# A gated attention followed by a multiplicative FFN: up products of the last three blocks in twenty products of parts

## The chip, the core and the metric

The kernel runs on one core of a Trainium2 chip. The metric is the device time of one execution in microseconds, the median of several runs. The names of the engines are those of the profile: PE is TensorE, DVE is VectorE, ACT is ScalarE, POOL is GpSimd, SP is the queue that issues the DMAs.

## The reference

All inputs are float32: q, k, v and f_logit of shape (4, 8, 768, 48), w1 and w2 of 384 x 1024, w3 of 1024 x 1024, w_out of 1024 x 384.

```python
f = 1.0 / (1.0 + np.exp(-f_logit))
for t in range(S):
    state = f[:, :, t, :, None] * state + np.einsum('bhd,bhe->bhde', k[:, :, t], v[:, :, t])
    y[:, :, t] = np.einsum('bhd,bhde->bhe', q[:, :, t], state)
x = attn_out.transpose(0, 2, 1, 3).reshape(B * S, H * D)   # 3072 x 384
h = ((x @ w1) * (x @ w2)) @ w3
return h @ w_out
```

## The kernel before

**Attention.** The 3072 tokens are 24 units of 128. Per unit VectorE makes two scans over the gates (L393, L415) and scales q and k (L409, L430); TensorE makes scores (L456) and transposes of k (L468); ScalarE copies the scores out of PSUM, GpSimd masks them (L549), TensorE multiplies with v (L490) and with the state (L509), makes the state's increment (L523), and VectorE updates the state (L638 to L644). The result is written to DRAM (L684) and gathered, transposed, into xt (L687). A unit's chain goes over four engines, so the gaps of TensorE in it are filled with products of the FFN.

**FFN.** The 24 units make six blocks of 512 tokens. w3 and w_out are multiplied into one matrix wc (L1176) early on. For each block, x is cut into 3 x 2 parts: three 128-row slices of the 384 features, two halves of 256 tokens. w1 and w2 are each cut into 3 x 8 tiles of 128 x 128. The function `seven` takes two of the eight column tiles and one of the two matrices: four outputs of 128 x 256 would take twelve products, and seven combinations of parts (m1 to m7, as Strassen's scheme does for a 2 x 2 x 2 part of it, with the third slice of features added in the plain way) make it eleven. Its sums are made by VectorE out of PSUM: u2 (L838), u3 (L841), c11, c22, c21, c12 (L847, L852), and for w2 the multiplication with the result of w1 (L856); ScalarE copies m1 (L817). The sums of parts of x (`sums`, L784) and of w (`sum_up`, L1208) are made on VectorE. Block 0 and half of block 1 use plain products (`part`). Every block ends in two `down` groups, each of seven combinations of four products of 192 columns, with four sums S0 to S3 before them (L950), and u2, u3, c22, c21, c12 after (L965, L978, L989, L995, L1003). All products go through `three` (L714), so they stand under one line in the profile.

**Order.** `Plan` takes every step with an engine, an assumed cost, a priority and its dependencies, and puts out a list for each engine; the hardware queues run in that order. `need(u)` is the due time of unit u. PSUM is two banks for scores (pa), two for values (py), and a pool of four banks, f, for the rest. A step that takes a bank names the step that frees it. After the last unit, a range check on VectorE (L1233 to L1241) decides whether a general path is to be taken at the end; it is not taken here.

Of the kernel before, what the change touches and what calls it, by code (L numbers as in the profile page):

```python
# [64 lines left out]
LOW = float.fromhex("0x1p-15")  # L67
HIGH = float.fromhex("0x1.dffffep+16")
LOOSE = 5
FULL = 35.0  # L70
FLOOR = 2.0**-60
RANGE = 2.0**-40


class Plan:
# [26 lines left out]
    def order(self):  # L102
# [12 lines left out]
        def places(t, name):  # L115

            ends = [(after(t, enders[id(h)]) if h else 0.0, i) for i, h in enumerate(self.pools[name])]
            return [e for e in ends if e[0] is not None]
# [88 lines left out]
def ranged(ctx, tc, q, k, f_logit, v, w1, w2, w3, w_out, out, ident, w12, wc, left):  # L207
# [7 lines left out]
    work = ctx.enter_context(tc.tile_pool(name="work", bufs=2))  # L215
    work3 = ctx.enter_context(tc.tile_pool(name="work3", bufs=3))
    abp = ctx.enter_context(tc.tile_pool(name="abp", bufs=4))
    outs = ctx.enter_context(tc.tile_pool(name="outs", bufs=4))
    one = ctx.enter_context(tc.tile_pool(name="one", bufs=1))
    dram = ctx.enter_context(tc.tile_pool(name="dram", bufs=3, space=bass.MemoryType.DRAM))  # L220
# [3 lines left out]
    floor = keep.tile([R, NQ], F32, name="floor")  # L224
    back = keep.tile([R, NQ], F32, name="back")
    gate = [keep.tile([R, NQ + 1], F32, name=f"gate{i}") for i in range(2)]
    qs, ks, fs = ([keep.tile([R, NQ], F32, name=f"{nm}{i}") for i in range(n)] for nm, n in (("q", 3), ("k", 2), ("f", 2)))
    masked = [keep.tile([P, 2, HP, C], F32, name=f"A{i}") for i in range(2)]
    sb = [keep.tile([R, HP, R], F32, name=f"sb{i}") for i in range(2)]
# [51 lines left out]
    def heads(t):  # L281
        return t.rearrange("p (h c) -> p h c", c=C)
# [44 lines left out]
    def need(u):  # L327
        return (0.0, 1.0, 2.0, 3.0)[u] if u < 4 else 60 + 14.5 * (u - 4)

# [22 lines left out]
    def front(u):  # L352
# [38 lines left out]
        def forward():  # L391
            s["P"] = one.tile([R, NQ], F32, name="fwd")
            nc.vector.tensor_tensor_scan(s["P"], gate[u % 2][:, 0:NQ], floor, 0.0, ALU.mult, ALU.max)  # L393
# [19 lines left out]
        def backward():  # L413
            s["R"] = one.tile([R, NQ], F32, name="bwd")
# [6 lines left out]
        def scale_k():  # L421
            s["K"] = work.tile([R, NQ], F32, name="K")
# [165 lines left out]
    def rest(u):  # L588
# [68 lines left out]
        def outcome():  # L657
            s["ys"] = work3.tile([R, HP, C], F32, name="ys")
# [51 lines left out]

    def three(out_, lhs, rhs, start=True):

        for i in range(len(lhs)):
            nc.tensor.matmul(  # L714
                out_, lhsT=lhs[i], rhs=rhs[i], start=start and i == 0, stop=i == len(lhs) - 1,
                skip_group_check=True,
            )

    def ffn(n):
# [187 lines left out]

        if n == 0:
            part(0, 2, range(KH))
# [10 lines left out]
        def down(i):  # L920
# [89 lines left out]

            n0 = 100 * n + 90 + i + 60 * (n > 1) + 30 * (n == NB - 2)

# [246 lines left out]
    for u in range(NU):  # L1259
# [363 lines left out]
```

## Time and profile before

| | |
|---|---|
| median of 3 runs | 490.2 us (490.07 to 490.37) |
| profiled execution | 490.37 us, its span 488.7 us |
| TensorE's granted clock | 0.998 |
| busy: PE, DVE, ACT, POOL | 477.4, 359.8, 166.2, 61.5 us |
| last unit's products with v begin | 298.13 us |
| last product's sum begins | 483.23 us |
| products through L714 of 256 columns, mean of a record | 0.379 us |
| products through L714 of 192 columns, mean of a record | 0.327 us |
| DVE sums 128x256 with a PSUM input (L852) | 0.42 us |
| DVE sums 128x512 from SBUF (L950) | 0.68 to 0.69 us |
| POOL masks 64x256 (L549), 80 of them | 0.578 us |

The page has one execution on the hardware. The share of busy time of each engine is given for the whole and for 40 slices of the span, as tenths. The chain is followed back from the last instruction to what released it. A product in float32 is two records on PE, and records overlap, so what a product costs is to be read from the starts of neighbouring records and not from a record's mean. "Idle before" is named with the engine whose instruction ended it.

### The profile page before, as it was taken

How to read it: one execution, taken by the hardware profiler on the slowest of the kernel's cores; microseconds unless marked ns; L12 is line 12 of the kernel's file. 1: busy time of each engine (PE TensorE's matmuls, PEld its weight loads, DVE VectorE, ACT ScalarE, POOL GpSimd, SP SyncE). 2: the span in 40 equal slices, each digit the busy share in tenths (PEclk: the TensorE clock that was granted, in tenths of full speed). 3: DMA queues.
4: the chain of work that ended last, by engine and by line, in shares of the span. 5: the costliest groups of instructions: out<-in, count | busy, mean ns of one | idle time of the engine just before them, and what ended most of it. 6: DMA issues, size and time to landing. Idle time of an engine off the chain costs nothing.

```text
span 488.7 us, 9559 instructions
## 1 busy us (share of the span) xinstructions
PE 477.4 (98%) x3696; PEld 408.0 (83%) x3696; DVE 359.8 (74%) x721; ACT 166.2 (34%) x380; POOL 61.5 (13%) x115
## 2 busy tenths in 40 slices
PE   7899999999999999999999999999999999999995
PEld 6788744666799888899988888988899888889994
DVE  7999899999997688688877866456763667655541
ACT  4688456573234442544433541001100110110010
POOL 9110000305202111221311201000000000000000
PEclk9999999999999999999999999999999999999999
DMA  5999367663326653346642113000011000000011
GB/s 176 297 334 262 100 243 258 211 184 82 82 79 166 164 138 106 90 124 165 166 124 51 34 25 91 32 34 0 20 48 50 16 1 0 1 1 1 32 62 43
DMA packets 44920, 50.00 MB, mean 102 GB/s; under 512 B 15426, under 2 KB 34370, under 8 KB 43842
## 3 DMA queue, kind: packets, MB, share of 16 engines
q1 hardware_dynamic: 44866, 49.30, 34.3%
q8 instruction: 31, 0.51, 0.4%
q14 instruction: 23, 0.19, 0.1%
HBM read 40.63 MB, written 8.65 MB: 101 GB/s over the span
## 4 chain that ended last, share of the span: by engine, by line
PE 86%; DVE 6%; issue 1%; DVEq 0%
PE f L714 69%; PE f L1176 4%; PE py L490 4%; PE pa L456 2%; PE py L509 2%; PE py L468 2%; DVE place L1208 1%; PE f L523 1%; DVE place L1123 1%; DVE place L1129 1%; DVE bwd L415 1%; PE f L692 1%; DVE fwd L393 1%; DVE place L1222 0%; DVE place L950 0%
## 5 line engine op out<-in xcount | busy, mean ns | idle before, releaser
L714 PE MATMUL f<-xt,w 128*128 128x256 f32 (+1 forms) x600 | 159.1, 396 | 0.0
L714 PEld LDWEIGHTS f<-xt,w 128*128 128x128 f32 x600 | 113.5, 190 | 24.7 <-issue 10.8
L714 PE MATMUL f<-place 128*128 128x192 f32 (+1 forms) x504 | 112.1, 350 | 0.3 <-DVE place L950 0.3
L714 PEld LDWEIGHTS f<-place 128*128 128x128 f32 x504 | 87.8, 190 | 6.4 <-DVE place L950 0.6
L549 POOL TENSOR_SCALAR_AFFINE_SELECT A<-A 64x256 f32<-64x256 f32 (+1 forms) x84 | 49.0, 604 | 232.1 <-PE py L468 106.0
L1176 PE MATMUL f<-place 128*128 128x384 f32 x128 | 42.6, 489 | 0.5 <-DVE place L1129 0.5
L817 ACT COPY a<-f 128x256 f32<-128x256 f32 x36 | 13.4, 373 | 81.5 <-PE f L714 69.6
L1176 PEld LDWEIGHTS f<-place 128*128 128x128 f32 x128 | 23.9, 190 | 17.3 <-DVE place L1129 1.1
L714 PE MATMUL f<-xt,place 128*128 128x256 f32 x144 | 37.1, 380 | 0.0
L714 PE MATMUL f<-wc,ab 128*128 128x192 f32 x192 | 35.1, 326 | 0.0
L714 PEld LDWEIGHTS f<-wc,ab 128*128 128x128 f32 x192 | 32.0, 190 | 0.4
L393 DVE TENSOR_TENSOR_SCAN fwd<-gate,floor 112x512 f32<-112x512 f32 x24 | 29.9, 1244 | 2.5 <-ACT gate L385 2.0
L543 ACT COPY A<-pa 64x256 f32<-64x256 f32 (+1 forms) x60 | 24.2, 439 | 20.2 <-PE pa L456 19.6
L415 DVE TENSOR_TENSOR_SCAN bwd<-gate,back 112x512 f32<-112x512 f32 x24 | 29.6, 1233 | 0.7
L714 PEld LDWEIGHTS f<-xt,place 128*128 128x128 f32 x144 | 26.6, 189 | 3.5 <-issue 0.2
L841 DVE TENSOR_TENSOR place<-f,a 128x256 f32<-128x256 f32 x36 | 15.2, 421 | 18.7 <-PE f L714 18.5
L653 ACT COPY sb<-S 48x192 f32<-48x192 f32 x40 | 14.0, 350 | 27.7 <-DVE S L644 18.2
L490 PEld LDWEIGHTS py<-A,vt 128*64 128x64 f32 (+1 forms) x320 | 17.5, 129 | 6.7 <-issue 6.2
L1112 ACT ACTIVATE place<-place 128x512 f32<-128x512 f32 (+2 forms) x24 | 21.3, 886 | 4.0 <-DVE w L1129 2.0
L490 PE MATMUL py<-A,vt 128*64 128x128 f32 x320 | 22.6, 281 | 0.0
L714 PE MATMUL f<-place,w 128*128 128x256 f32 x72 | 21.4, 379 | 0.0
L1115 ACT ACTIVATE place<-place 128x512 f32<-128x512 uint32 (+2 forms) x24 | 21.3, 893 | 0.0
(119 smaller groups left out, 632.7 us busy)
## 6 DMA issues: line engine op xcount, KB each, us to landing
place<-in_w_dram SPq DMA_DIRECT2D x8, 1024.0 KB, 4.9
place<-in_w_dram SPq DMA_DIRECT2D x12, 512.0 KB, 9.4
out_dram<-o SPq DMA_DIRECT2D x24, 192.0 KB, 1.9
q<-in_q_dram SPq DMA_DIRECT2D x46, 96.0 KB, 2.4
f<-in_f_logit_dram SPq DMA_DIRECT2D x44, 96.0 KB, 2.3
k<-in_k_dram SPq DMA_DIRECT2D x44, 96.0 KB, 2.3
yt<-ys SPq DMA_DIRECT2D x40, 96.0 KB, 2.1
xt<-yt SPq DMA_DIRECT2D x20, 192.0 KB, 2.7
```

The costliest lines, as they stand in the source:

```text
L393: nc.vector.tensor_tensor_scan(s["P"], gate[u % 2][:, 0:NQ], floor, 0.0, ALU.mult, ALU.max)
L415: nc.vector.tensor_tensor_scan(s["R"][:, ::-1], gate[u % 2][:, NQ:0:-1], back[:, ::-1], 0.0, ALU.mult, ALU.max)
L490: nc.tensor.matmul(y_block(u, b)[64 * half : 64 * half + w], lhsT=s["v"][:, h * D : h * D + w], rhs=s["A"][:, par, hp], start=zone not in ...
L543: nc.scalar.copy(parts_of(s["A"].rearrange("p r h c -> p (r h c)"))[p0:p1, :, f], parts_of(s["pa"].rearrange("p r n -> p (r n)"))[p0:p1, : ...
L549: nc.gpsimd.affine_select(out=a, in_=a, pattern=pattern, compare_op=ALU.is_ge, fill=0.0, base=0, channel_multiplier=-1,)
L653: nc.scalar.copy(sb[u % 2][rows(par), :, 64 * par : 64 * par + D], s["S"][rows(par)])
L714: nc.tensor.matmul(out_, lhsT=lhs[i], rhs=rhs[i], start=start and i == 0, stop=i == len(lhs) - 1, skip_group_check=True,)
L817: nc.scalar.copy(q["a"], q["X"])
L841: nc.vector.tensor_tensor(ups["u3", k], q["Y"], q["a"], ALU.add)
L1112: nc.scalar.activation(m, hi.bitcast(F32), AF.Abs)
L1115: nc.scalar.activation(lo.bitcast(F32), lo, AF.Copy, bias=2.0, scale=2.0**-51)
L1176: nc.tensor.matmul(w3s["p", jc], lhsT=w3s[jc][:, kc * P : kc * P + P], rhs=wos[:, kc], start=(kc == 0), stop=(kc == KF - 1),)
```

## The change

The up products of blocks 3, 4 and 5 are no longer made by `seven`. The new function `twenty` takes one matrix (w1 or w2) and four of the eight column tiles. It sees x as 3 x 2 parts and w as 3 x 4 parts, so that eight outputs of 128 x 256 would take 24 products, and makes them with twenty. TWENTY names for each product which part or sum of x and of w it multiplies; X_SUMS and W_SUMS say how the 13 sums of x (128 x 256 each, per block) and the 23 sums of w (128 x 512 each, once) are made; both run on VectorE. STEPS lists products (p) and the sums that follow: with an operand in PSUM (a name in b) on VectorE, copies (=) on ScalarE, sums of SBUF values alone on GpSimd. Of the final multiplications of w1's result with w2's, the even outputs go to GpSimd, the odd ones to VectorE.

- These three blocks are planned behind all units of attention, and `twenty` waits for the last unit. The due times of the units are closer, 12 apart and not 14.5. The gather of block 5 is issued when block 3's products are done.
- Its results stand in five halls of PSUM: the banks of pa and py, and one bank of the pool f, which leaves three to the down groups.
- The sums lie in the places of the attention's tensors, which are joined into one tile (chunked), and of `place`. A sum of w that needs a place of the attention's waits for the attention's end; the others wait for block 2's up products, whose sums of w they overwrite.
- Attention itself, blocks 0 to 2, and all down groups are computed as before; the priorities of the down groups change.

```diff
+X_SUMS = (
+    "6 0 - 2", "7 1 - 2", "8 6 + 3", "9 3 + 4", "10 7 + 4", "11 7 - 3", "12 9 - 5", "13 6 + 1",
+    "14 8 - 5", "15 1 + 4", "16 0 + 3", "17 6 - 4", "18 10 - 5",
+)
+W_SUMS = (
+    "12 0 - 4", "13 12 + 5", "14 1 + 9", "15 13 - 1", "16 12 - 6", "17 14 - 16", "18 17 + 10", "19 12 - 14",
+    "20 11 + 3", "21 18 + 20", "22 15 + 7", "23 16 - 1", "24 22 - 3", "25 18 + 11", "26 0 + 8", "27 26 - 14",
+    "28 13 + 7", "29 19 + 7", "30 16 + 2", "31 17 - 8", "32 21 + 2", "33 19 - 20", "34 4 + 8",
+)
+TWENTY = (
+    (11, 16), (7, 12), (10, 19), (12, 23), (13, 0), (6, 24), (5, 18), (14, 25),
+    (4, 15), (9, 27), (8, 21), (13, 28), (15, 29), (3, 30), (12, 31), (16, 32),
+    (2, 33), (17, 22), (18, 17), (2, 34),
+)
+STEPS = (
+    "p b0 1 1", "= v0 b0", "p b1 4 1", "p b1 19 0", "- o0 b1 v0", "p b2 0 1", "- v1 v0 b2",
+    "p b3 17 1", "p b4 8 1", "= v2 b4", "+ v3 b3 v2", "+ v4 v3 v0", "p b5 5 1", "- v5 v3 b5",
+    "p b6 16 1", "- v6 v5 b6", "p b7 10 1", "- v7 b7 v5", "p b8 13 1", "= v8 b8", "+ v9 v8 b7",
+    "p b9 6 1", "+ v10 b9 v8", "p b9 7 0", "- o7 v7 b9", "- v11 v1 v9", "p b6 15 0", "+ o2 v11 b6",
+    "p b10 2 1", "p b11 12 1", "= v12 b10", "- v13 v12 b11", "- o3 v6 v13", "- v14 v13 v4", "p b12 11 1",
+    "+ o1 v14 b12", "p b13 18 1", "+ v15 b13 v12", "- v16 v1 v15", "+ v17 v16 v2", "p b14 3 1", "- o5 v17 b14",
+    "- o6 v10 v16", "p b15 9 1", "p b15 14 0", "+ o4 v16 b15",
+)
+LATE = 3
...
+def first_use(side, d):
+    order = [TWENTY[int(r.split()[2])][side] for r in STEPS if r[0] == "p"]
+    above = [first_use(side, int(r.split()[0])) for r in (X_SUMS, W_SUMS)[side] if str(d) in r.split()[1::2]]
+    return min([i for i, x in enumerate(order) if x == d] + above)
...
+    chunked = keep.tile([P, 23 * NQ], F32, name="chunked")
+    spots = [chunked[:, i * NQ : i * NQ + NQ] for i in range(23)]
+    floor, back, *spare = [x[0:R] for x in spots[4:]]
+    qs, ks, fs, k_in, q_in, y_in = (
+        [spare.pop() for _ in range(n)] for n in (3, 2, 2, 2, 3, 3)
+    )
+    one_p, one_r = spare.pop(), spare.pop()
+    masked = [chunked[:, 2 * i * NQ : 2 * i * NQ + 2 * NQ].rearrange("p (r h c) -> p r h c", r=2, h=HP) for i in range(2)]
...
+    w_at, after = {}, []
+    keeps = sorted({w for _, w in TWENTY if w >= 12}, key=lambda w: first_use(1, w))
+    soon = [at(2 * TH * i, 2 * TH) for i in range(12)] + spots[23 - len(spare) :]
+    w_at.update(zip(keeps, soon))
+    later = spots[: 23 - len(spare)]
+    for w in keeps[len(soon) :]:
+        w_at[w] = later.pop()
+        after.append(w)
+    ends = [at(a + 2 * TH * i, 2 * TH) for a in (9216, 12864) for i in range(2)]
+    w_at.update(zip([int(r.split()[0]) for r in W_SUMS if int(r.split()[0]) not in w_at], ends))
+    late_v = [t[:, i * TH : i * TH + TH] for t in later + ends for i in range(2)]
+    late_x = [[late_v.pop(0) for _ in X_SUMS] for _ in range(2)]
...
+    plan.pool("h", 5)
+    plan.pool("v", len(late_v))
...
-        return (0.0, 1.0, 2.0, 3.0)[u] if u < 4 else 60 + 14.5 * (u - 4)
+        return (0.0, 1.0, 2.0, 3.0)[u] if u < 4 else 60 + 12 * (u - 4)
...
-            s["Q"] = work3.tile([R, NQ], F32, name="Q")
+            s["Q"] = q_in[u % 3]
...
-        before = blk[n - 2]["up"] if n >= 2 else []
         if u < NPE:
             t["z"] = plan.add("PE", 1.6, moved, [t["y"]], n0 - 996, takes=["f"], frees=[moving])
-            t["x"] = plan.add("ACT", 0.55, settled, [t["z"]] + before, n0 - 20, frees=[t["z"]])
+            t["x"] = plan.add("ACT", 0.55, settled, [t["z"]], n0 - 20, frees=[t["z"]])
         else:
             t["z"] = moves(2, 197, 250, written, [t["y"]], n0 - 100)
-            t["x"] = moves(1, 197, 250, gathered, [t["z"]] + before, n0 - 100)
-
+            def gather():
+                t["x"] = moves(1, 197, 250, gathered, [t["z"]] + (blk[n - 2]["up"] if n >= 2 else []), n0 - 100)
+            if n < LATE + 2:
+                gather()
+            else:
+                t["gather"] = gather
+    halls, late_w, late_q = {}, [], []
+    def hall():
+        nm, i = ("pa", "py", "f")[plan.got // 2], plan.got % 2
+        if nm not in halls:
+            halls[nm] = ps.tile([P, 2, NQ], F32, name=nm)
+        return halls[nm][:, i, 0:TH]
+    def claimed():
+        halls["f"] = bank().unsqueeze(1)
+    def w_part(i, which=None):
+        if i >= 12:
+            t = w_at[i].rearrange("p (w t c) -> p w t c", w=2, t=2)
+        else:
+            kc, c = divmod(i, 4)
+            b, a = divmod(c, 2)
+            t = w12.rearrange("p w k (a b c) -> p w k a b c", b=2, c=P)[:, :, kc, 2 * a : 2 * a + 2, b]
+        return t if which is None else t[:, which]
+    def prepare():
+        ended = [tk[u]["z"] for u in range(NU - 3, NU)] + [tk[NU - 1][nm] for nm in ("v", "y", "c")]
+        halls["claim"] = plan.add("PE", 0.0, claimed, ended, 0, takes=["f"])
+        there = [x for p in pieces.values() for x in p] + blk[LATE - 1]["up"] + enders(LATE - 1)
+        tasks = {}
+        for row in sorted(W_SUMS, key=lambda r: first_use(1, int(r.split()[0]))):
+            d, x, op, y = row.split()
+            d, x, y = int(d), int(x), int(y)
+            def emit(d=d, x=x, y=y, op=op):
+                nc.vector.tensor_tensor(w_part(d), w_part(x), w_part(y), ALU.add if op == "+" else ALU.subtract)
+            tasks[d] = plan.add("DVE", 0.69, emit, [tasks[i] for i in (x, y) if i in tasks] + there + ended * (d in after), 100 * LATE + 20 + 0.01 * len(tasks))
+        return tasks
...
+        def x_sums():
+            tasks = {}
+            deps = [tk[n * UB + c]["x"] for c in range(UB)]
+            if n < LATE + 2:
+                deps += [tk[u]["z"] for u in range(NU - 3, NU)] + [tk[NU - 1][nm] for nm in "vyc"]
+            else:
+                deps += blk[n - 2]["last"]
+            for row in sorted(X_SUMS, key=lambda r: first_use(0, int(r.split()[0]))):
+                d, x, op, y = row.split()
+                d, x, y = int(d), int(x), int(y)
+                def emit(d=d, x=x, y=y, op=op):
+                    nc.vector.tensor_tensor(x_part(d), x_part(x), x_part(y), ALU.add if op == "+" else ALU.subtract)
+                tasks[d] = plan.add("DVE", 0.43, emit, [tasks[i] for i in (x, y) if i in tasks] + deps, 100 * n + 30 + 0.01 * len(tasks))
+            return tasks
+        def twenty(t, which, sums_):
+            n0 = 100 * n + 50 + 8 * t + 4 * which
+            tiles = [c + 2 * t for c in (0, 4, 1, 5)]
+            ready = [tk[n * UB + c]["x"] for c in range(UB)] + [tk[NU - 1][nm] for nm in "myv"] + [halls["claim"]]
+            last = takes_ab(tiles[0], plan.add("PE", 0.0, lambda: None, ready + late_q[-1:], n0))
+            made, homes, opened, read = {}, {}, {}, {}
+            def result(o):
+                return a_b(tiles[o % 4])[:, o // 4 * TH : o // 4 * TH + TH]
+            started = None
+            def step(row):
+                nonlocal last, started
+                kind, to, *of = row.split()
+                if kind == "p":
+                    i = int(of[0])
+                    x, w = TWENTY[i]
+                    start = of[1] == "1"
+                    def emit():
+                        if start:
+                            homes[to] = hall()
+                        lhs = w_part(w, which)[:, t] if w >= 12 else up_weights(w12, which, w // 4, tiles[w % 4])
+                        three(homes[to], [lhs], [x_part(x)], start)
+                    deps = [last, sums_.get(x), late_w[0].get(w)] + read.get(to, [])
+                    last = plan.add("PE", 0.43, emit, deps, n0, takes=["h"] if start else [])
+                    made[to] = last
+                    if start:
+                        opened[to] = last
+                    s["up"].append(last)
+                    if len(s["up"]) % len(TWENTY) == len(TWENTY) // 2:
+                        started = last
+                    return
+                here = to[0] == "o" and which == 0
+                eng = "ACT" if kind == "=" else "DVE" if "b" in of[0] + of[1] else "POOL"
+                def emit():
+                    if here:
+                        homes[to] = result(int(to[1:]))
+                    else:
+                        homes[to] = late_v[plan.got]
+                    if kind == "=":
+                        nc.scalar.copy(homes[to], homes[of[0]])
+                        return
+                    e = nc.vector if eng == "DVE" else nc.gpsimd
+                    e.tensor_tensor(homes[to], homes[of[0]], homes[of[1]], ALU.add if kind == "+" else ALU.subtract)
+                cost = {"ACT": 0.38, "DVE": 0.43, "POOL": 1.1}[eng]
+                made[to] = plan.add(
+                    eng, cost, emit, [made[i] for i in of] + ready_v, n0 - 200, takes=[] if here else ["v"],
+                    frees=[opened[i] for i in of],
+                )
+                opened[to] = made[to]
+                for i in of:
+                    read.setdefault(i, []).append(made[to])
+                if to[0] == "o":
+                    o = int(to[1:])
+                    if which == 0:
+                        first_of[t, o] = made[to]
+                    else:
+                        def times():
+                            (nc.vector if o % 2 else nc.gpsimd).tensor_tensor(result(o), result(o), homes[to], ALU.mult)
+                        s["done"][t].append(plan.add("DVE" if o % 2 else "POOL", 0.43 if o % 2 else 1.1, times, [made[to], first_of[t, o]], n0 - 190, frees=[made[to]]))
+            ready_v = ready + [tk[u]["z"] for u in range(NU - 3, NU)] + list(late_w[0].values())
+            for row in STEPS:
+                step(row)
+            late_q.append(started)
...
+        first_of = {}
+        if n >= LATE:
+            if not late_w:
+                late_w.append(prepare())
+            sums_ = x_sums()
+            for t in range(2):
+                for which in range(2):
+                    twenty(t, which, sums_)
+            s["last"] = s["up"][-1:]
+        elif n == 0:
...
-            n0 = 100 * n + 90 + i + 60 * (n > 1) + 30 * (n == NB - 2)
+            n0 = 100 * n + 90 + i + 75 * (n > 0) + 90 * (n >= LATE - 1)
...
-        if u % UB == UB - 1:
+        if u % UB == UB - 1 and u // UB < LATE:
             ffn(u // UB)
+    for n in range(LATE, NB):
+        for u in range(n * UB, n * UB + UB):
+            if "gather" in tk[u]:
+                tk[u]["gather"]()
+        ffn(n)
```

More of the change, by code (lines that the diff above doesn't have):

```diff
@@ L115, in places @@
         def places(t, name):
-            ends = [(after(t, enders[id(h)]) if h else 0.0, i) for i, h in enumerate(self.pools[name])]
+            ends = [(after(t, enders.get(id(h), [{"end": None}])) if h else 0.0, i) for i, h in enumerate(self.pools[name])]
             return [e for e in ends if e[0] is not None]
@@ L215, in ranged @@
     work = ctx.enter_context(tc.tile_pool(name="work", bufs=2))
-    work3 = ctx.enter_context(tc.tile_pool(name="work3", bufs=3))
     abp = ctx.enter_context(tc.tile_pool(name="abp", bufs=4))
     outs = ctx.enter_context(tc.tile_pool(name="outs", bufs=4))
-    one = ctx.enter_context(tc.tile_pool(name="one", bufs=1))
-    dram = ctx.enter_context(tc.tile_pool(name="dram", bufs=3, space=bass.MemoryType.DRAM))
+    dram = ctx.enter_context(tc.tile_pool(name="dram", bufs=12, space=bass.MemoryType.DRAM))
     ps = ctx.enter_context(tc.tile_pool(name="ps", bufs=1, space=PSUM))
     ps_f = ctx.enter_context(tc.tile_pool(name="ps_f", bufs=1, space=PSUM))
-    floor = keep.tile([R, NQ], F32, name="floor")
-    back = keep.tile([R, NQ], F32, name="back")
+    chunked = keep.tile([P, 23 * NQ], F32, name="chunked")
[6 more added lines that the diff above has]
+    masked = [chunked[:, 2 * i * NQ : 2 * i * NQ + 2 * NQ].rearrange("p (r h c) -> p r h c", r=2, h=HP) for i in range(2)]
     gate = [keep.tile([R, NQ + 1], F32, name=f"gate{i}") for i in range(2)]
-    qs, ks, fs = ([keep.tile([R, NQ], F32, name=f"{nm}{i}") for i in range(n)] for nm, n in (("q", 3), ("k", 2), ("f", 2)))
-    masked = [keep.tile([P, 2, HP, C], F32, name=f"A{i}") for i in range(2)]
     sb = [keep.tile([R, HP, R], F32, name=f"sb{i}") for i in range(2)]
@@ L391, in forward @@
         def forward():
-            s["P"] = one.tile([R, NQ], F32, name="fwd")
+            s["P"] = one_p
             nc.vector.tensor_tensor_scan(s["P"], gate[u % 2][:, 0:NQ], floor, 0.0, ALU.mult, ALU.max)
@@ L413, in backward @@
         def backward():
-            s["R"] = one.tile([R, NQ], F32, name="bwd")
+            s["R"] = one_r
             nc.vector.tensor_tensor_scan(
@@ L421, in scale_k @@
         def scale_k():
-            s["K"] = work.tile([R, NQ], F32, name="K")
+            s["K"] = k_in[u % 2]
             if u < NPE:
@@ L657, in outcome @@
         def outcome():
-            s["ys"] = work3.tile([R, HP, C], F32, name="ys")
+            s["ys"] = heads(y_in[u % 3])
             py = s["yb"] if u < NPE else s["py"][0:R, :, 0 : 2 * C]
@@ L717, in three, with enders @@
             )
+    def enders(n):
+        return [q[nm] for q in blk[n]["seven"] for nm in ("e12", "e21", "e22")]
     def ffn(n):
@@ L906, in seven, with x_part @@
             s["up"] += [q[nm] for nm in ("m1", "m2", "m7", "m4", "m3")]
-        if n == 0:
+        def x_part(i):
+            return late_x[n % 2][i - 6] if i >= 6 else quarter(i % KM, i // KM)
+        def x_sums():
[12 more added lines that the diff above has]
+            return tasks
```

## Prediction

> **What bounds the kernel now.** I read the page first (shares, then slices), then the busy table by stretches of 50 us, then single instructions in the timeline.
>
> ```profile
> PE 477.4 (98%) x3696; PEld 408.0 (83%) x3696; DVE 359.8 (74%) x721; ACT 166.2 (34%) x380; POOL 61.5 (13%) x115
> ...
> PE   7899999999999999999999999999999999999995
> ...
> DVE  7999899999997688688877866456763667655541
> ...
> POOL 9110000305202111221311201000000000000000
> ...
> PE 86%; DVE 6%; issue 1%; DVEq 0%
> ```
>
> TensorE is full in nearly every slice, and 86% of the chain that ended last is on it. GpSimd does nothing after about 295 us. The busy table has the columns PE, PEld, DVE, ACT, POOL:
>
> ```profile
> 250.00:300.00 50.00, 50.00 (x533) 43.75 (x534) 38.38 (x87) 21.20 (x57) 8.98 (x20) 1.00 0.23 57
> 300.00:350.00 50.00, 50.00 (x258) 45.94 (x258) 27.98 (x73) 5.29 (x15) 0.00 (x0) 1.00 0.07 21
> 350.00:400.00 50.00, 50.00 (x261) 46.09 (x260) 30.19 (x72) 5.00 (x14) 0.00 (x0) 1.00 0.10 32
> 400.00:450.00 50.00, 50.00 (x240) 44.46 (x239) 30.82 (x73) 5.86 (x16) 0.00 (x0) 1.00 0.00 0
> ```
>
> Attention ends at 300 us. From there to 483 us TensorE runs products alone without a gap, VectorE is about 60% busy. So the tail is bound by the number of products. A busy PE need not be at its peak, so I take prices from start to start:
>
> ```profile
> 350.45 1.03 PE L714 MATMUL f<-xt,place 128*128 128x256 f32 x4
> 351.31 0.59 PE L714 MATMUL f<-place,w 128*128 128x256 f32 x2
> ...
> 357.79 1.46 PE L714 MATMUL f<-wc,ab 128*128 128x192 f32 x8
> 359.09 3.09 PE L714 MATMUL f<-place 128*128 128x192 f32 x18
> ```
>
> Each product is two records. Two products 256 wide take 351.31 - 350.45 = 0.86 us, so 0.433 each; four 192 wide take 1.30, so 0.325 each. VectorE, from start to start:
>
> ```profile
> 351.51 0.42 DVE L852 TENSOR_TENSOR a<-f,a 128x256 f32<-128x256 f32 x1 [0.31 <-PE f L714]
> 351.97 0.42 DVE L856 TENSOR_TENSOR ab<-ab,a 128x256 f32<-128x256 f32 x1
> ...
> 352.83 0.43 DVE L856 TENSOR_TENSOR ab<-ab,place 128x256 f32<-128x256 f32 x1
> 353.17 0.42 DVE L838 TENSOR_TENSOR place<-f,a 128x256 f32<-128x256 f32 x1
> 353.51 0.68 DVE L950 TENSOR_TENSOR place<-ab 128x512 f32<-128x512 f32 x1
> 354.22 0.69 DVE L950 TENSOR_TENSOR place<-place,ab 128x512 f32<-128x512 f32 x1
> ```
>
> An instruction that needs the result of the one before follows after 0.46 us (256 wide) or 0.71 (512), one that does not after 0.34; for 512 wide the trace has 0.60 (470.24 to 470.85). For 192 wide I use 0.28 and 0.39 in the same way.
>
> [...] No run shows GpSimd at a sum yet. [...]
>
> ```profile
> 292.71 1.98 POOL L549 TENSOR_SCALAR_AFFINE_SELECT A<-A 64x256 f32<-64x256 f32 x4 [11.21 <-PE f L714]
> 292.74 0.65 DVE L856 TENSOR_TENSOR ab<-ab,place 128x256 f32<-128x256 f32 x1
> ```
>
> ```profile
> L856 DVE TENSOR_TENSOR ab<-ab,place x36: 424/425/678, 180.1 to 447.9; 128x256 f32<-128x256 f32 x36
> ```
>
> The product of two SBUF tensors (L856) took 0.65 us beside GpSimd and 0.425 in the median; over the nine L856 that I found beside GpSimd the mean is 0.55, the worst 0.68. VectorE sums with one PSUM input (L852) stay at 0.42 beside GpSimd. [...]
>
> **The change part by part.**
>
> *Products removed.* Blocks 3 to 5 had eight times eleven products of 256 columns each, 88; now four times twenty, 80. 3 x 8 x 0.433 = 10.4 us off TensorE. Those of the last block stand in the tail, those of block 3 partly beside attention; but as TensorE is full in both, all of it counts. Everything else on TensorE keeps its count.
>
> *Reordering of the first 300 us.* Due times are closer (12 instead of 14.5), the up products of blocks 0 to 2 and five of their six down groups fill the gaps of attention. The stretch from 80 to 135 us has VectorE at 95%, so a wrong order could cost there. I summed VectorE's work up to each unit's backward scan against TensorE's up to its scores, in the orders of both programs: VectorE is behind by at most 10.6 us before (unit 6) and 10.3 after (unit 8). Cost 0, bounds -1 and +1.
>
> *Weight sums at the turn to the tail.* 23 sums 128x512 on VectorE, 0.60 or 0.72 each. They overwrite places that block 2's products read, so they can't start before those end. I put T0 at the end of unit 21's group on TensorE. From T0 TensorE has 4 products of 256 (1.7), 20 of 192 (6.5), unit 22 (2.7: 287.87 to 290.58 is the same group before), 20 of 192 (6.5), unit 23 (1.6: 298.13 to 299.77), 28 of 192 (9.1): ready for the first of the twenty products at T0+28.15. VectorE starts its first weight sum at T0+6.1. Up to the two sums S0 and S1 of the next down group it has 16 weight sums (9 x 0.60 + 7 x 0.72 = 10.4), four sums of the down groups and unit 22's state (2.2), S0 and S1 (1.3), and 0.5 of waits for TensorE: T0+20.5. The down product m6 needs S1 and TensorE was ready for it at 19.05: 1.5 us lost. Then VectorE has the range check (1.0), two sums (1.2), seven weight sums (4.3) and five of the down group (1.6), with 0.3 of waits: T0+28.85; TensorE's down products end at 29.65, and the first x sum is there by 29.2. So 1.5 us, bounds 0 and 4. Queued behind S1 on VectorE is all of this; nothing else waits.
>
> *Sums of the products.* Per twenty products 15 sums with a PSUM input on VectorE, 7 sums of SBUF values on GpSimd, 4 copies on ScalarE (0.373 each, L817; ScalarE is 10% busy, so nothing). Half of the final multiplications go to GpSimd too. Per block 13 x sums instead of 4. In total per block VectorE goes from 60 to 81 instructions. From T0+28.85, VectorE's work in its new order against TensorE's, after each group of twenty products (us, cumulative; n counts VectorE's instructions with two SBUF inputs):
>
> group 1: VectorE 9.8, TensorE 8.7, n 12; group 2: 20.1, 17.3, 21; group 3: 29.6, 28.5, 31; group 5: 48.6, 49.7, 46; group 6: 57.7, 61.0, 56; group 8: 75.0, 86.1, 66.
>
> TensorE may run ahead by the five PSUM halls, six products or 2.6 us, less 0.3 for the way between engines; VectorE starts 0.7 late. The loss after a group is then 0.7 + VectorE + n e - TensorE - 2.3, with e the mean delay by the port. Group 2 gives 1.2 + 21 e, group 3 -0.5 + 31 e, group 6 -4.9 + 56 e; later groups give less, as down products come in. At e = 0.12 (the trace's 0.13 beside GpSimd; longer GpSimd sums, but not always one there) the worst is group 2, 3.7 us, which includes the 1.5 from the turn. At e = 0 it is 1.5; at e = 0.25, the trace's worst, group 6 gives 9.1.
>
> *GpSimd.* 108 instructions. [...] What waits is VectorE: o2, o5, o4 and o1 read GpSimd's results and stand in VectorE's queue before sums that free halls. I take 1.0 us for such waits, bounds 0 and 4.
>
> *End.* The last 92 down products (29.9 us) have three banks instead of four; each product's sum lies one product of 1.30 us ahead, against 0.36 for a sum: 0.
>
> Sum: 490.4 (the profiled execution; span 488.7 and 1.7 around it) - 10.4 + 3.7 + 1.0 = 484.7. The median of the runs shown is 0.2 lower, so 484.6 rounded.
>
> **Rivals.** *Full gain, 480.3* (490.2 - 10.4 + 0.5): VectorE's lag stays inside the halls and the port costs nothing. For it: L852 is untouched beside GpSimd. Against: groups 1 to 3 have more VectorE work than TensorE work whatever e is. Chance 0.12. *Gain eaten, 489.9*: e = 0.25, 9.1 + 1.0 lost. Chance 0.11. *Slower, 495.5*: the port. [...] then e = 0.35, and VectorE becomes the bound of the tail's first six groups: -4.9 + 56 x 0.35 = 14.7, and 490.2 - 10.4 + 14.7 + 1.0. It decides from e = 0.26 on, where 9.7 + 1.0 lost is more than the 10.4 gained. Against it: the trace's worst is 0.25. Chance 0.15. *GpSimd as the bound, 500*: at 1.4 us its 108 instructions take 151 us, started 4 us late, against 135 + 4.7: 15.5 more than the forecast. From 1.2 us on it leads. Against it: the select of 1024 elements took only 1.11 us. Chance 0.07.
>
> **How the numbers follow.** Forecast 0.55, between 481.5 and 488.5; it and the full gain, with a part of the eaten gain, make faster 0.72; same 0.07 (within 0.2%, which is about what a measurement of this kernel can tell from no change); slower 0.21. The range goes from 480.0, the full gain, to 493.0, into the slower port case, and leaves out 0.18.
>
> **What would show it.** Right: the PE tail in 40 slices still full but with small gaps just after attention, in which DVE is the releaser; VectorE at 90% or more for the first 50 us of the tail, then less; the x sums, whose inputs are both in SBUF, longer than 0.42[...]. Wrong: gaps of PE between 80 and 135 us; GpSimd sums over 1.1 us; waits of TensorE spread over the whole tail; or a tail without any gap.

## The result and the profile after

| | before | after |
|---|---|---|
| median | 490.26 us (490.07 to 490.37, 4 runs) | 509.56 us (509.03 to 509.94, 4 runs) |
| ratio | | 1.0393, interval 1.0375 to 1.0411 |
| profiled execution, its span | 490.37, 488.7 us | 509.03, 507.0 us |

The change makes the kernel 19.3 us slower; the forecast was 5.6 us faster. The shares and slices of the page after:

```profile
PE 479.6 (95%) x3648; PEld 394.6 (78%) x3648; DVE 403.6 (80%) x807; ACT 170.5 (34%) x392; POOL 146.1 (29%) x223
...
PE   8899999999999999999999989888989899999994
...
DVE  7999899999996777879788897778887766666641
...
POOL 9200000332222111111211111455554555265400
...
PE 80%; DVE 10%; issue 2%; ACT 1%; POOL 0%; DVEq 0%; ACTq 0%
```

The 48 records of the 24 products are gone (3696 to 3648), and yet PE is busy longer. From about 290 to 405 us its slices are eights and nines in turn, and the chain runs over DVE for 10% and not 6%. The busy table after, with the columns PE, PEld, DVE, ACT, POOL:

```profile
250.00:300.00 50.00, 48.64 (x551) 44.52 (x550) 42.08 (x91) 20.23 (x54) 9.85 (x20) 1.00 0.29 80
300.00:350.00 50.00, 44.89 (x204) 34.69 (x205) 39.27 (x94) 5.48 (x15) 18.83 (x24) 1.00 0.05 13
350.00:400.00 50.00, 43.06 (x198) 34.48 (x197) 42.20 (x92) 6.13 (x17) 26.51 (x34) 1.00 0.08 24
400.00:450.00 50.00, 47.91 (x233) 40.28 (x232) 33.58 (x78) 6.17 (x17) 24.52 (x33) 1.00 0.05 16
```

Read the counts, not the busy time: from 300 to 350 us TensorE issues 204 records instead of 258, and VectorE isn't full either. A product that starts after a stop has a longer record here (0.70 us and not 0.59 for its two), so busy time hides waiting. I therefore sum gaps from start to start: what lies between the starts of neighbouring products beyond 0.433 or 0.325 us. From 309 to 470 us that is 26.3 us after, against 0.7 in the whole tail before; the last 92 down products have none. Single waits of PE are short and many, 25 of them with 13.2 us in all; the answer on waits between 309 and 470 us (total us, times, longest):

```profile
PE pa L810 <- ACT chunked L1073: 2.3, 3, 1.7
PE pa L810 <- DVE place L1076: 2.0, 6, 0.6
PE pa L810 <- DVE ab L1076: 1.8, 3, 1.3
PE py L810 <- ACT place L1073: 1.8, 1, 1.8
...
PE f L810 <- DVE place L1076: 0.9, 1, 0.9
```

Nearly all are products into pa and py, which hold four of the five halls. Groups of VectorE and GpSimd in the same stretch (busy us, mean ns | idle before):

```profile
L1023 DVE TENSOR_TENSOR chunked<-chunked,xt 128x256 f32<-128x256 f32 x24 | 13.8, 589 | 0.1
...
L1092 DVE TENSOR_TENSOR ab<-ab,place 128x256 f32<-128x256 f32 x13 | 8.0, 612 | 0.6 <-POOL place L1076 0.5
```

```profile
L1076 POOL TENSOR_TENSOR place<-place,chunked x13: 716/727/1058, 333.1 to 464.4; 128x256 f32<-128x256 f32 x13
```

What the prediction calls the port is a delay of VectorE's instructions with two SBUF inputs beside GpSimd's. The delay is there: x sums and final multiplications of 0.42 us alone (L784 and L856 before, from 300 us on, with GpSimd idle) take 0.6 in the mean, while VectorE's sums with a PSUM input (L1076) stay at 0.41 to 0.42. What makes the delay no trace shows; "port" is a name for it here and no more. A GpSimd sum or multiplication takes 0.73 us in the median of the 108, 0.80 in the mean.

### The profile page after: what moved, and what is told of

It reads as the page before. It is cut to its first block, busy times and chain, and to the rows that moved or that the text cites. A ratio compares the mean times of both kernels' runs of the same rounds, so it can differ in the third digit from the quotient of the medians.

```text
span 507.0 us, 9758 instructions
## 1 busy us (share of the span) xinstructions
PE 479.6 (95%) x3648; PEld 394.6 (78%) x3648; DVE 403.6 (80%) x807; ACT 170.5 (34%) x392; POOL 146.1 (29%) x223
## 4 chain that ended last, share of the span: by engine, by line
PE 80%; DVE 10%; issue 2%; ACT 1%; POOL 0%; DVEq 0%; ACTq 0%
PE f L810 46%; PE pa L810 8%; PE f L1378 7%; PE py L810 6%; PE py L541 4%; PE pa L507 3%; DVE place L1076 3%; DVE chunked L1023 2%; PE py L560 2%; PE py L519 2%; DVE chunked L1076 1%; PE f L574 1%; DVE place L1152 1%; DVE ab L1076 1%; DVE ab L1092 1%
## 5 line engine op out<-in xcount | busy, mean ns | idle before, releaser
L600 POOL TENSOR_SCALAR_AFFINE_SELECT chunked<-chunked 64x256 f32<-64x256 f32 (+1 forms) x84 | 49.2, 606 | 231.7 <-issue 71.5
L810 PE MATMUL f<-xt,w 128*128 128x256 f32 (+1 forms) x360 | 94.7, 408 | 0.0
L810 PEld LDWEIGHTS f<-xt,w 128*128 128x128 f32 x360 | 68.0, 190 | 19.3 <-issue 10.8
L810 PE MATMUL f<-place 128*128 128x192 f32 (+1 forms) x360 | 71.6, 338 | 1.8 <-DVE place L1152 1.4
L810 PEld LDWEIGHTS f<-place 128*128 128x128 f32 x360 | 60.9, 190 | 5.0 <-DVE place L1152 1.6
L1378 PEld LDWEIGHTS f<-place 128*128 128x128 f32 x128 | 23.9, 190 | 17.3 <-DVE place L1331 1.1
L444 DVE TENSOR_TENSOR_SCAN chunked<-gate,chunked 112x512 f32<-112x512 f32 x24 | 29.5, 1231 | 3.0 <-ACT gate L436 2.6
L594 ACT COPY chunked<-pa 64x256 f32<-64x256 f32 (+1 forms) x60 | 24.2, 439 | 20.1 <-PE pa L507 19.4
L466 DVE TENSOR_TENSOR_SCAN chunked<-gate,chunked 112x512 f32<-112x512 f32 x24 | 29.5, 1228 | 0.7
L810 PE MATMUL pa<-chunked,place 128*128 128x256 f32 x74 | 22.8, 392 | 4.3 <-ACT chunked L1073 1.9
L810 PE MATMUL py<-chunked,place 128*128 128x256 f32 x66 | 20.2, 390 | 3.3 <-ACT place L1073 1.8
L541 PE MATMUL py<-chunked,vt 128*64 128x128 f32 x320 | 22.6, 281 | 0.0
```

What stands on the lines that cost most here:

```text
L466: nc.vector.tensor_tensor_scan(s["R"][:, ::-1], gate[u % 2][:, NQ:0:-1], back[:, ::-1], 0.0, ALU.mult, ALU.max)
L541: nc.tensor.matmul(y_block(u, b)[64 * half : 64 * half + w], lhsT=s["v"][:, h * D : h * D + w], rhs=s["A"][:, par, hp], start=zone not in ...
L594: nc.scalar.copy(parts_of(s["A"].rearrange("p r h c -> p (r h c)"))[p0:p1, :, f], parts_of(s["pa"].rearrange("p r n -> p (r n)"))[p0:p1, : ...
L600: nc.gpsimd.affine_select(out=a, in_=a, pattern=pattern, compare_op=ALU.is_ge, fill=0.0, base=0, channel_multiplier=-1,)
L810: nc.tensor.matmul(out_, lhsT=lhs[i], rhs=rhs[i], start=start and i == 0, stop=i == len(lhs) - 1, skip_group_check=True,)
L1378: nc.tensor.matmul(w3s["p", jc], lhsT=w3s[jc][:, kc * P : kc * P + P], rhs=wos[:, kc], start=(kc == 0), stop=(kc == KF - 1),)
```

## The experiments

Theories at the start: the *port* (GpSimd's sums delay VectorE's instructions with two SBUF inputs); *lockstep* (five halls and queues in a planned order, with too little play); *GpSimd's latency*; the *order alone*. Ratios are to the kernel before, timed together with each run (490.31 to 490.45 us).

### What it is not, and how much is the port

**e1.** The late blocks keep their new place but are made by `seven`.

```diff
-        if n >= LATE:
+        if n > NB:
...
+            s["last"] = s["up"][-1:]
```

> Blocks 3 to 5 stand behind the attention as in the change, but their up products are made by seven (eleven products) as before; no sum is on GpSimd. If the loss is in the twenty products and their sums (the port, or the lockstep of engines), the order alone costs nothing: 489 to 492 us. If the moved order and the closer due times cost (the fourth theory), it is well over 495 us.

Measured 491.22 us, ratio 1.0017 (1.0010 to 1.0025); 0.8 us of gaps in the tail, against 0.7 in the kernel before. The order costs 0.8 us.

**e2.** GpSimd's instructions in the twenty products cover 16 columns and not 256, except the sums that write a result of w1; the rest of these sums and multiplications is left out. (The same cut in the final multiplications, and the memsets that set the places to zero, are not printed.)

```diff
+                    m = TH if eng == "DVE" or here else 16
-                    e.tensor_tensor(homes[to], homes[of[0]], homes[of[1]], ...)
+                    e.tensor_tensor(homes[to][:, 0:m], homes[of[0]][:, 0:m], homes[of[1]][:, 0:m], ...)
```

> Every instruction of GpSimd on SBUF values in the twenty products covers 16 columns and not 256, except the sums that write a result of w1; so most of these sums and final multiplications are left out in all but 16 columns. Order, waits and all instructions of VectorE, ScalarE and TensorE stay; GpSimd sets the places to zero once, between 300 and 309 us, about 20 instructions that may hold VectorE for 1 to 3 us there. Port theory: VectorE's instructions with two SBUF inputs fall back to 0.42 us and most of the 26 us of TensorE's gaps go with it: 486 to 491 us. Lockstep theory (five halls, queues in an order planned at other costs): gaps stay, 500 to 508 us. GpSimd's own latency as the cause would look like the port in time, but then VectorE's x sums would have been at fault in nothing: they tell the two apart, since they wait for no GpSimd result.

Measured 501.84 us, ratio 1.0231 (1.0213 to 1.0248). VectorE's multiplications fell back to 0.42 us, and 7.7 us of the kernel's time went. Gaps of 19.2 us stayed: the port is a part, not the whole cause.

**e3, e4, e5.** Ten halls, two in a bank, planned anew; all sums on VectorE; and ten half-bank halls in the order of the change.

```diff
-        nm, i = ("pa", "py", "f")[plan.got // 2], plan.got % 2
+        got = plan.got % 5 * 2 + plan.got // 5
+        nm, i = ("pa", "py", "f")[got // 4], got // 2 % 2
...
-        return halls[nm][:, i, 0:TH]
+        return halls[nm][:, i, got % 2 * TH : got % 2 * TH + TH]
...
-    plan.pool("h", 5)
+    plan.pool("h", 10)
```

> Two halls of 256 columns in each of the five banks, ten and not five; nothing is left out. Port theory in its plain form (VectorE has too much to do): TensorE may run 2.2 us further ahead, so 2 to 4 us are gained, 505 to 508 us. Lockstep theory (short bursts of VectorE, each longer than five halls cover, with idle time of VectorE between them): most of the gaps close, 490 to 498 us.

```diff
-                eng = "ACT" if kind == "=" else "DVE" if "b" in of[0] + of[1] else "POOL"
+                eng = "ACT" if kind == "=" else "DVE"
```

> All sums and final multiplications that were on GpSimd are on VectorE, in a plan made for that. 108 more instructions on VectorE of about 0.40 us, 43 us, less the 15 us by which it is now held: VectorE has 28 us more to do in the tail than in the change, where it idles some 45 of 161 us. Port theory: VectorE full through the tail, 508 to 520 us. If waiting for results of GpSimd is what costs, it is faster than the change: under 505 us.

```diff
+        used[plan.got] = 1 - used.get(plan.got, 1)
+        c0 = used[plan.got] * TH
-        return halls[nm][:, i, 0:TH]
+        return halls[nm][:, i, c0 : c0 + TH]
```

> The order of the change exactly, but each of the five halls alternates between the two halves of its bank, so that TensorE may open a hall while its earlier contents are still read. All instructions are those of the change[...]. If TensorE is held by halls that come free late, most of the 26 us of gaps close: 486 to 500 us. If it is held by VectorE's time as such (the x sums and weight of its queue), little: 505 to 509 us. If two engines in one bank get into each other's way, it is slower than the change, over 512 us.

Measured: e3 521.65 us (it computes other values than the change and is read for its time alone), e4 535.05, e5 509.14. Ten halls planned anew cost 12 us more than five, where both theories had expected a gain. With the order kept they gain nothing: PE's slices are those of the change, digit for digit. e4 is slower than either theory had it. Its x sums and multiplications, with GpSimd idle, took 0.42 us each, but the waits before down groups grew to 6.9 us. At its stops of 2.31, 4.08, 6.9 and 4.93 us the trace has TensorE's clock at half, for 20.5 us together; that is an estimated 10 us at most of the 25.5 that e4 lost against the change. So GpSimd's help is worth having, and more halls, as they lie here, close no gap.

**e6, e7.** The x sums cut short, alone and together with e2's edit.

```diff
-                nc.vector.tensor_tensor(x_part(d), x_part(x), x_part(y), ...)
+                nc.vector.tensor_tensor(x_part(d)[:, 0:16], x_part(x)[:, 0:16], x_part(y)[:, 0:16], ...)
```

> The order of the change, but each of the 39 x sums covers 16 columns and not 256; the rest of these sums is left out (the places are set to zero once by GpSimd, by 300 us). GpSimd works as in the change. VectorE has 39 times about 0.5 us less to do, 19 us. If VectorE's time is what sets the tail, the gaps shrink nearly by as much: 492 to 498 us. If the way between the engines (latency, halls) does, the gaps stay: over 503 us.

> The two edits together: GpSimd's instructions and the x sums on 16 columns, the rest of these sums left out; same order. No hold by the port and 17 us less for VectorE than without the port. If VectorE's time and the port together are the cause: 482 to 488 us, near the full gain of 480. If halls and latency are a cause of their own, 8 us or more of gaps remain: 490 to 497 us.

Measured 504.03 and 511.40 us. VectorE is busy for 12 us less in e6 (391.8 against 403.6), and the time fell by 5.5 us; with e2's edit it rose, which neither reading had expected. e7's loss lies at the turn (13 us of gaps up to 340 us, against 6.5 in e2). There a weight sum of VectorE waited 3.21 us for GpSimd, which was setting places to zero; a down product then stood 3.10 us, and TensorE's clock was at half for 10.24 us from 311.83 us on. From 340 us on its gaps are 13.1 us, e2's 12.6, with or without x sums. VectorE's time as the main cause falls.

**e8.** The x sums on GpSimd, planned anew (`nc.vector` becomes `nc.gpsimd` in `x_sums`, cost 0.8).

> Nothing is left out: the 39 x sums are on GpSimd and no longer on VectorE, and the plan is made anew with 0.8 us for an instruction of GpSimd (measured) instead of 1.1. VectorE loses 39 instructions of 0.66 us, 26 us; GpSimd gains 39 of 0.75, to 147 instructions, 112 us in a tail of 170. If VectorE's time is the cause: 485 to 492 us, as fast as before or faster. If GpSimd's results become what is waited for: 495 to 505 us.

Measured 506.09 us, slower than both readings had it: 18.5 us of gaps, although VectorE has 39 instructions less.

### A wait that nobody planned

What was left could be seen in the first products of the tail. After:

```profile
309.04 0.59 PE L810 MATMUL pa<-chunked,place 128*128 128x256 f32 x2
309.47 0.70 PE L810 MATMUL pa<-chunked,w 128*128 128x256 f32 x2
310.21 0.37 ACT L1073 COPY chunked<-pa 128x256 f32<-128x256 f32 x1 [0.65 <-PE pa L810]
310.63 0.70 PE L810 MATMUL pa<-xt,place 128*128 128x256 f32 x2 [0.46 <-ACT chunked L1073]
```

By STEPS these are b0 and b1, then v0 as a copy of b0, then the second product into b1. It needs nothing of v0. Yet the copy starts only after b1's first product, and b1's second product only after the copy. b0 and b1 are two halls, in two banks, but in one tile: pa. In the built program I compared every wait of TensorE in the tail with the places that the instructions really share. Of 118 waits for VectorE 63 are for a reader of the other hall of the tile, of 44 waits for ScalarE 21; VectorE and ScalarE wait for TensorE in that way too. Hall f, alone in its tile, has none; with ten halls in these tiles (e3) TensorE's are 79 and 31. That fits e3 and e5, whose ten halls lie in the same tiles and brought nothing.

**e9, e10.** Each hall in a PSUM tile of its own; e10 with e2's edit as well.

```diff
+    passing = ctx.enter_context(ExitStack())
+    ps = passing.enter_context(tc.tile_pool(name="ps", bufs=1, space=PSUM))
...
         halls["f"] = bank().unsqueeze(1)
+        passing.close()
+        halls["own"] = passing.enter_context(tc.tile_pool(name="own", bufs=1, space=PSUM))
...
-        nm, i = ("pa", "py", "f")[plan.got // 2], plan.got % 2
-        if nm not in halls:
-            halls[nm] = ps.tile([P, 2, NQ], F32, name=nm)
-        return halls[nm][:, i, 0:TH]
+        if plan.got == 4:
+            return halls["f"][:, 0, 0:TH]
+        return halls["own"].tile([P, TB], F32, name=f"h{plan.got}")[:, 0:TH]
```

> Nothing is left out; order, instructions and places as in the change, but each hall is a PSUM tile of its own. In the change two halls lie in one tile (pa, and py), and 63 of TensorE's 118 waits for VectorE and 21 of its 44 waits for ScalarE in the tail are for the reader of the other hall of the tile; here none is. If these waits are what is left when the port is taken away (19 of the 26 us of gaps): 489 to 496 us. If they cost little: over 504 us.

> Halls in tiles of their own and GpSimd's instructions on 16 columns, the rest of its sums and multiplications left out (its sums that write a result of w1 are whole). No hold by the port, no wait for a neighbour hall. If these two are the whole cause: 481 to 486 us, the full gain of 480 and the turn to the tail of 1 to 2 us. If VectorE's time or the latency is a third cause: over 488 us.

Measured: e9 **488.78 us**, ratio 0.9966 (0.9958 to 0.9974); e10 483.52, ratio 0.9858 (0.9841 to 0.9874). The same four instructions in e9 (`three` is L812 there):

```profile
309.50 0.59 PE L812 MATMUL h<-chunked,place 128*128 128x256 f32 x2
309.94 0.70 PE L812 MATMUL h<-chunked,w 128*128 128x256 f32 x2
310.19 0.37 ACT L1075 COPY chunked<-h 128x256 f32<-128x256 f32 x1 [0.17 <-PE h L812]
310.47 0.59 PE L812 MATMUL h<-xt,place 128*128 128x256 f32 x2
```

The copy comes 0.69 us after b0's start instead of 1.17, and the third product starts 0.53 us after the second instead of 1.16. The waits of PE from 309 to 470 us in e9:

```profile
PE h L812 <- DVE ab L1078: 2.4, 3, 0.8
PE f L812 <- DVE place L1078: 0.4, 1, 0.4
PE h L812 <- ACT place L1075: 0.4, 1, 0.4
PE h L812 <- DVE chunked L1078: 0.3, 1, 0.3
```

Gaps fell from 26.3 to 6.1 us, and with GpSimd cut short as well to 1.3. Tiles are worth 20.8 us, cutting GpSimd short 5.3 more; in the other order it is 7.7 (e2) and then 18.3.

**e15, e16.** Does it take the twenty products? The kernel *before*, with its four banks f in two shared tiles, and as a control in four tiles that are made once too.

```diff
-        return ps_f.tile([P, TB], F32, name=f"f{plan.got}")
+        nm, i = f"g{plan.got // 2}", plan.got % 2
+        if nm not in banks:
+            banks[nm] = ps_f.tile([P, 2, TB], F32, name=nm)
+        return banks[nm][:, i]
```

> The kernel before, nothing left out, but its pool of four banks is two tiles of two banks each; same order, same places. 139 of TensorE's 208 waits for VectorE in the FFN, and 47 of 70 for ScalarE, are then for the reader of the other bank of the tile. If sharing a tile is the cause as such, it is much slower than before, 505 us or more. If the waits need the twenty products, it stays at 490 to 492 us.

> The control: the kernel before with four tiles of one bank each, made once as in the one before. If sharing is what costs there and not that the tiles are made once: 489.5 to 491.5 us.

Measured: e15 **536.92 us**, ratio 1.0953 (1.0935 to 1.0972); e16 490.48, ratio 1.0002 (0.9993 to 1.0011). Sharing as such costs the kernel before 46 us. The page of e15, then of e16:

```profile
PE 499.1 (93%) x3696; PEld 404.4 (76%) x3696; DVE 358.0 (67%) x721; ACT 164.6 (31%) x380; POOL 60.0 (11%) x115
...
PE   8999999979999999989989999989999998999995
```

```profile
PE 478.4 (98%) x3696; PEld 408.8 (84%) x3696; DVE 360.0 (74%) x721; ACT 166.1 (34%) x380; POOL 61.9 (13%) x115
...
PE   8899999999999999999999999999999999999994
```

These waits come from how the program is built, tile by tile: pa's halls lie in two banks, and e9 and e16 run without such waits. Whether the halves of a bank in e3 and e5 would have to wait for each other in tiles of their own too, no run here shows.

### Closing the rest

**e11, e12, e13, e14.** e9 with x sums on GpSimd: all of them (e11, e12), or only those of blocks 4 and 5 (e13, e14); with half of the final multiplications on VectorE (e11, e13), or none (e12, e14). GpSimd's instructions are planned at 0.8 us. The edit of e13, in part:

```diff
-                    nc.vector.tensor_tensor(x_part(d), x_part(x), x_part(y), ...)
+                    (nc.vector if n == LATE else nc.gpsimd).tensor_tensor(x_part(d), x_part(x), x_part(y), ...)
```

> Nothing is left out: halls in tiles of their own, the 39 x sums on GpSimd, plan with 0.8 us for GpSimd. The port can then hold only VectorE's final multiplications (24) and the sums before the down groups. If the two causes are the whole: 480 to 486 us, faster than both kernels. If GpSimd (147 instructions, 112 us) is waited for: 488 to 496 us.

> As the one before, but all 48 final multiplications on GpSimd too, 171 instructions of 0.75 us, 128 us. Port theory: VectorE has only the sums before the down groups left to be held, so 1 to 3 us faster than the one before. If GpSimd, full at 75 to 80% of the tail, delays the multiplications that the down groups wait for, it is slower than the one before by 1 to 6 us.

> Nothing is left out: halls in tiles of their own; the x sums of block 3 on VectorE as in the change, those of blocks 4 and 5 on GpSimd, plan with 0.8 us for GpSimd. If the stop at the turn and the low clock after it are what the version with all x sums on GpSimd lost (4.4 us and about 3): 481 to 485 us. If the port holds VectorE as much through more of GpSimd's work: 487 to 490 us.

> As the one before, with all final multiplications on GpSimd. VectorE then has in the tail, from block 4 on, only the sums before the down groups that the port can hold: the same as the one before within 1 us if its gaps are closed already, 1 to 2 us faster if they are not.

Measured: 488.47, 488.82, 488.06 (ratio 0.9947, 0.9931 to 0.9964) and 488.47 us: at most 0.7 us better than e9. The 480 to 486 us of the better reading (e11, e13) did not come; the times lie in the range of the other one. The gaps after 320 us are closed (0.5 us in e13). VectorE waited for GpSimd's results ten times there, 6.6 us in all, without such gaps; so what e10 took away is rather GpSimd's hold on VectorE than results of GpSimd that come late. But the turn has a new stop. e13, single instructions and then stretches of 4 us (the columns after the counts are the clock, the DMA share and GB/s):

```profile
298.67 5.23 POOL L1025 TENSOR_TENSOR chunked<-chunked,xt 128x256 f32<-128x256 f32 x5 [1.42 <-PE py L542]
300.17 1.20 DVE L1154 TENSOR_TENSOR place<-ab 128x512 f32<-128x512 f32 x1
301.41 1.09 DVE L1154 TENSOR_TENSOR place<-place,ab 128x512 f32<-128x512 f32 x1
302.56 7.21 PE L812 MATMUL f<-place 128*128 128x192 f32 x24 [3.46 <-DVE place L1154]
```

```profile
300.00:304.00 4.00, 1.44 (x5) 1.44 (x5) 3.86 (x10) 0.00 (x0) 3.92 (x5) 0.74 0.23 53
304.00:308.00 4.00, 4.00 (x14) 4.00 (x14) 3.59 (x6) 0.00 (x0) 4.00 (x4) 0.50 0.02 0
308.00:312.00 4.00, 4.00 (x24) 4.00 (x23) 3.35 (x7) 0.00 (x0) 2.51 (x3) 0.90 0.00 0
```

GpSimd's x sums, one behind the other, draw VectorE's sums of 0.68 us out to 1.09 and 1.20. The down product m6 so waits 3.46 us and not 1.36, and then TensorE's clock is at half: twelve products take 7.04 us (to 309.60) instead of 3.9. That is 2.1 and 3.1 us, about the 4.5 us that e13 lacks to e10. Here the clock fell 2.84 us into the stop, and it fell at or just after stops of 3.10 us (e7), 2.71 (e15) and 2.31 (e4) too. It stayed at full speed through the 1.36 us of e9 and through stops of up to 1.76 us in the change.

**e17, e18.** e13 and e14, but the x sums of blocks 4 and 5 are to wait for the weight sums.

```diff
+            if n > LATE:
+                deps += list(late_w[0].values())
```

> Halls in tiles of their own, x sums of blocks 4 and 5 on GpSimd, but only after the weight sums; nothing is left out. If the stop at the turn and the low clock after it were what was lost: no stop over 1.5 us at 300 us, clock 0.99 or more, and 481 to 484.5 us. If the port in the tail costs as much as in the change: 486 to 489 us.

> As the one before, with all final multiplications on GpSimd: within 1 us of it if VectorE's gaps are closed, with GpSimd not waited for; over 1 us slower if the down groups wait for GpSimd's multiplications.

Measured 488.77 and 488.68 us; the edit did not move the sums. The plan put the sums at 308 us, but the chip ran them from 295.62: they share no data with the weight sums, so the built program has no wait, and GpSimd's queue had nothing ahead of them. m6 again stood 3.45 us. So e17's time says nothing on the port, though it lies in the range given for it. Whether the stop at the turn is all that is missing stays open: it is argued from e13's numbers, not shown.

## Why the prediction was wrong

- **Products removed, 10.4 us**: right as far as the runs can tell. e10, which has neither shared tiles nor long GpSimd sums, comes to within 3.2 us of the 480.3 that the prediction calls the full gain.
- **Reordering, 0 in bounds of 1**: right, 0.8 us (e1).
- **Turn, 1.5 us**: right. m6 stood 1.36 us, and the first of the twenty products began 10.6 us after unit 23's group, as forecast (T0+29.65 against T0+19.05).
- **Sums of the products, 3.7 us**: here it failed, in the words "TensorE may run ahead by the five PSUM halls, six products or 2.6 us". The halls were taken for five independent buffers because the change calls them so. Four of them lie in two tiles, so TensorE, VectorE and ScalarE wait for each other at every turn between neighbours, and each late sum reaches TensorE at once. That is 20.8 us (e9). It also breaks the form of the sum: I took the largest lag after a group, which is right if the halls even out what lies between; without that play, losses add up. The gaps run from 309 to 470 us, which fits, but no run tests the form of the sum alone. Its 0.3 us for the way between engines was an estimate; in e9 the copy of b0 starts 0.26 us after the product's end (0.69 - 0.433 us from its start).
- **The port in that sum, e = 0.12**: the delay came, its size was off. VectorE's multiplications and x sums took 0.63 us in e9, so e is 0.21; with that the forecast's own formula gives 6.9 us for group 6. e9 lost 8.9 us of the 10.4 (488.8 against 490.3 - 10.4), 0.8 of them by the order. Cutting GpSimd short brings 5.3 us with tiles apart and 7.7 with them shared.
- **GpSimd, 1.0 us of waits**: close. VectorE waited 1.3 us for it; a sum took 0.73 us in the median, up to 1.18, which no trace of the kernel before could show. **End, 0**: right.
- **Rivals**: slower was right in sign, but by another cause than the one named. The port would have needed e = 0.35, which was the author's estimate and is in no trace; in the change x sums and multiplications were 0.21 us longer in the mean (309 to 470 us), and the gaps were not in VectorE's full stretches. The sign that the text gave for being wrong, waits of TensorE spread over the whole tail, is what came.

In sum: 490.3 - 10.4 + 20.8 (tiles) + 5.3 (port) + 0.8 (order) + 1.4 (turn) + 1.3 (gaps that e10 still has) = 509.5, measured 509.56. The 20.8 and 5.3 are differences of the runs themselves, so the test of this sum is the rest of it: 483.4, against 483.52 in e10. The faster versions that follow leave nothing out: e9, 1.6 us below the kernel before and 20.8 below the change, and e13, 2.3 us below the kernel before.

## What to carry to other kernels

A buffer counts as one of many only if the program waits for it alone: before five places are priced as five, look in which tile each lies, and check one product in the trace against what it really reads. Where waits are short, many and on engines that aren't full, compare the waits with the data before pricing any engine. And a dependency in a plan orders nothing on the chip unless the two steps share data or a queue, as in e17, where sums planned at 308 us ran from 295.62.

## What the runs showed of the hardware

- GpSimd's memsets did not hold VectorE: in e2 VectorE's sums of two SBUF inputs ran beside them at their usual length, 0.68 and 0.69 us.

```profile
296.56 0.68 DVE L801 TENSOR_TENSOR place<-place,w 128x512 f32<-128x512 f32 x1
296.65 1.07 POOL L778 MEMSET place<- 128x256 f32 x4
297.27 0.69 DVE L801 TENSOR_TENSOR place<-place 128x512 f32<-128x512 f32 x1
```

- A GpSimd sum of 16 columns still takes 0.22 to 0.33 us in the mean of its groups (e2), against 0.73 for 256, so a sixteenth of the columns still takes 30% of the time or more.
- A stop of TensorE of 3.46 us cost 3.1 us more after it, by the clock (e13); one of 1.36 us cost only itself (e9). From 40 us on and up to the last product, each stretch at half clock lasted 3.41 (as in e14), 6.83 (e13) or 10.24 us (e7), after stops of 2.31 to 6.9 us; the longest stretch followed a stop of 3.10 us (e7).
